# Linear attention with a gated feed-forward: reciprocal denominators replicated through DRAM, and half-chunk products of two pairs of tiles in one array mode

## The chip, the cores and the metric

The kernel runs on one core of a Trainium2 chip. The metric is device time in microseconds, the median of several executions. All executions quoted here are fast, at a mean granted TensorE clock of 0.99 to 1.00. A ratio is the mean time of one kernel's fast runs over the mean of the other kernel's fast runs of the same rounds, so it is not quite the ratio of the medians that stand beside it.

## The reference, cut to what matters

```python
xn = _layernorm(x)                                  # x: 1 x 2048 x 640, bf16
q, k, v = split_heads(xn @ wqkv)                    # 32 heads of 20
phi = lambda t: where(t > 0, t + 1, exp(t)) + 1e-6
kv  = einsum("bhsd,bhse->bhde", phi(k), v)
z   = einsum("bhsd->bhd", phi(k))
num = einsum("bhqd,bhde->bhqe", phi(q), kv)
den = einsum("bhqd,bhd->bhq", phi(q), z)[..., None] + 1e-6
s   = merge_heads(num / den) @ wo
g   = silu(relu(xn @ w1) @ w2)                      # w1: 640 x 1728, w2: 1728 x 640
return x + s * g
```

Two facts matter. The division by `den` is one number per head and token, and the kernel applies it to phi(q), whose 640 features lie on partitions: each of the 32 reciprocals has to be repeated over the 20 features of its head. And 1728 is 13 x 128 + 64, so the product with `w2` has a last chunk of 64 rows, half of the array.

## The kernel before

A small scheduler gives every operation a count on its engine and makes readers and overwriters wait for counts. If PE writes a bank that an earlier counted group of PE wrote, and nothing has told PE since that this group is done, PE waits for its own count.

In what follows PE is TensorE, DVE is VectorE, ACT is ScalarE, POOL is GpSimd, and SP is the engine that issues the DMAs. A bank is one of the eight 512-column pieces of PSUM, into which PE writes. A full matmul uses all 128 rows of the array. Blocks are named after their result: an H block is five matmuls of the product with `w1`, a G block is xn^T phi(k) for 128 features, a kv block multiplies that by the weights of v, and a W block multiplies kv by `wo`.

Features on partitions (`pqT`, phi(q) transposed, five chunks of 128), then the denominators. `den` leaves the reciprocals of 32 heads and 4 blocks of 512 tokens on 128 partitions (`rden`). They are spread to features by a matmul with a 0/1 matrix, one 32-row matmul per token block, and multiplied into `pqT` by DVE:

```python
def expand(m):
    fns = [(lambda eng, i=i: eng.matmul(ps[4 + i], lhsT=EmQ[H * i:H * (i + 1), m, :],
                                        rhs=rden[H * i:H * (i + 1), :], start=True, stop=True)) for i in range(J)]
    sc.group("PE", fns, ...)
    for i in range(J):
        sc.op("DVE", lambda eng, i=i: eng.tensor_tensor(out=pqT[:, m, schunk(i)], in0=pqT[:, m, schunk(i)],
                                                        in1=ps[4 + i], op=ALU.mult), ...)
...                                   # [cut]
for k in range(C):                    # C = 5
    lastG = G_block(k, gb[k % 2])     # 32 full matmuls: xn^T phi(k)
    expand(k)
```

The gate. `U(p)` computes the product with `w2` for a pair of token tiles, then four 64-row half products (two token tiles x two halves of the output), then two Silus. Output tiles (`s_tile`) of the previous pair run between its parts:

```python
def U(p, hook=None):
    ...                                                          # [cut: 26 full matmuls per output half n]
        if n == 0:
            sc.group("PE", fns, R=Rh, W=[("ps", bs[0]), ("ps", bs[0] + 1)])
            if hook is not None:
                hook()
    for n in range(2):
        for u in range(2):
            fns.append(lambda eng, u=u, n=n: eng.matmul(
                ps[bs[n] + u][:, 0:HN], lhsT=hTl[64 * u:64 * (u + 1), jp, P * q:P * (q + 1)],
                rhs=w2l[64 * u:64 * (u + 1), HN * n:HN * (n + 1)], start=False, stop=True))
    sc.group("PE", fns, R=..., W=[("ps", bs[n] + u) for n in range(2) for u in range(2)])
    for n in range(2):
        ...                                                      # [cut: Silu of output half n on ACT]
```

## Time and profile before

| | before |
|---|---|
| median time | 229.53 us |
| profiled span | 227.5 us |
| PE busy | 97% |
| share of PE in the chain that ended last | 93% |
| DVE, ACT, POOL busy | 47%, 39%, 20% |

Three lines of the page of the kernel before: span, busy time by engine (share of the span, number of instructions), and the chain that ended last by engine.

```profile
span 227.5 us, 3552 instructions
...
PE 221.0 (97%) x1474; PEld 134.8 (59%) x1484; DVE 108.1 (47%) x202; ACT 88.1 (39%) x145; POOL 46.1 (20%) x63
...
PE 93%; DVE 3%; DMA 2%; issue 1%; POOL 0%; SPq 0%; ACT 0%
```

PE is the limit. Only what shortens its stream of instructions, or the few microseconds after it, can shorten the run.

The chain in order of time (start, us, what) of the kernel before, at the expansions. L692 is a G block, L680 an expansion, L742 the first product with `w2`.

```profile
112.47 4.45 PE psT L692 x32
116.92 0.33 PE psT L680 x4
117.25 4.45 PE psT L692 x32
...
136.04 0.33 PE psT L680 x4
136.37 3.64 PE psT L742 x26
```

One G block and one expansion repeat every 4.78 us. At the steady pitch of full 320-column matmuls (26 in 3.53 us, 0.1358 us each) 32 of them take 4.345 us, so an expansion costs 0.435 us, not the 0.33 of its own line.

The timeline of the kernel before at one group of half products (L752); PEld is the weight load, in brackets the idle time before it and what ended it.

```profile
167.96 0.11 PEld L752 LDWEIGHTS psT<-reg,hTl 64*128 64x128 bf16 x4 [0.26 <-issue]
167.97 0.45 PE L752 MATMUL psT<-reg,hTl 64*128 64x320 bf16 x4
168.34 0.52 PEld L770 LDWEIGHTS psT<-reg,pqT 128*128 128x128 bf16 x5 [0.26 <-issue]
```

Weight loads otherwise follow each other closely (16.2 us of idle before the 416 loads of L742, 0.04 us each on the mean); going into the 64-row mode and coming out of it they stand idle for 0.26 us each time. The chain gives the price of the whole group. A pair of tiles repeats every 10.27 us, and its 72 full matmuls take 72 x 0.1358 = 9.78, so a group of four costs 0.48 us, or 0.96 us for two groups:

```profile
168.03 0.38 PE psT L752 x4
...
178.30 0.38 PE psT L752 x4
```

The timeline of the kernel before at its end: L770 are the last two output tiles, L759 the two Silus of the last pair, L784 the gate multiply, L787 the last add of the residual.

```profile
221.02 2.89 PE L770 MATMUL psT<-reg,pqT 128*128 128x320 bf16 x20
221.13 1.30 ACT L759 ACTIVATE reg<-psT 128x640 bf16<-128x640 f32 x2 [10.32 <-PE psT L752]
222.59 0.82 DVE L784 TENSOR_TENSOR reg<-psT,reg 128x640 bf16<-128x640 f32 x1 [4.02 <-PE psT L770]
...
225.14 0.32 DVE L787 TENSOR_TENSOR reg<-reg 128x320 bf16<-128x320 bf16 x1
```

From the start of the last products to the end of the last add: 225.14 + 0.32 - 221.02 = 4.44 us.

### The profile page before, as it was taken

Reading aid. Unit: us, or ns where it says so; the run is one execution under the profiler, and the core shown is the slowest. Engines: PE = TensorE matmul, PEld = TensorE weight load, DVE = VectorE, ACT = ScalarE, POOL = GpSimd, SP = SyncE. Lnnn points to the kernel's source line nnn. Section 1 sums busy time; section 2 is a strip of 40 time slices with the busy share of each in tenths; the row PEclk is TensorE's granted clock in tenths of the full one; section 3 lists DMA queues with packets and bytes.
Section 4 is the critical chain, followed back from the end, with each engine's and each line's share of the span. In section 5 each row is a group of like instructions: output and inputs, shape, how many; then the busy total and the mean of one; then the engine's idle time right before and its main releaser. Section 6 shows DMA issues by size and latency. Waiting matters only on the chain.

```text
span 227.5 us, 3552 instructions
## 1 busy us (share of the span) xinstructions
PE 221.0 (97%) x1474; PEld 134.8 (59%) x1484; DVE 108.1 (47%) x202; ACT 88.1 (39%) x145; POOL 46.1 (20%) x63
## 2 busy tenths in 40 slices
PE   7899999999999999999999999999999999999993
PEld 7664555455554555444466667666767676676762
DVE  3799911896549852945134446111323222222244
ACT  2898665567665667554511122322020202021011
POOL 2357642312632267700000004000000000000000
PEclk9999999999999999999999999999999999999999
DMA  6999900012401160000097009400100011000011
GB/s 206 325 397 232 242 4 0 0 30 58 32 1 29 29 61 22 0 0 3 5 331 214 0 0 297 168 0 3 58 32 29 29 55 35 29 29 32 29 58 58
DMA packets 20895, 17.95 MB, mean 79 GB/s; under 512 B 8880, under 2 KB 20880, under 8 KB 20880
## 3 DMA queue, kind: packets, MB, share of 16 engines
q1 hardware_dynamic: 20880, 17.74, 27.8%
q8 instruction: 11, 0.18, 0.4%
q14 instruction: 4, 0.03, 0.0%
HBM read 13.03 MB, written 2.62 MB: 69 GB/s over the span
## 4 chain that ended last, share of the span: by engine, by line
PE 93%; DVE 3%; DMA 2%; issue 1%; POOL 0%; SPq 0%; ACT 0%
PE psT L742 25%; PE psT L514 24%; PE psT L692 10%; PE psT L491 9%; PE psT L770 9%; PE psT L439 8%; DMA reg<-in_A_x_dram 2%; PE psT L719 2%; PE psT L752 1%; DVE stats L394 1%; PE psT L527 1%; DVE reg L784 1%; PE psT L680 1%; PE psT L704 1%; PE psT L602 1%
## 5 line engine op out<-in xcount | busy, mean ns | idle before, releaser
L742 PE MATMUL psT<-reg,hT 128*128 128x320 bf16 x416 | 59.1, 299 | 0.1
L514 PE MATMUL psT<-reg 128*128 128x512 bf16 x252 | 56.8, 379 | 0.5 <-issue 0.2
L742 PEld LDWEIGHTS psT<-reg,hT 128*128 128x128 bf16 x416 | 40.5, 98 | 16.2 <-PE psT L742 0.4
L514 PEld LDWEIGHTS psT<-reg 128*128 128x128 bf16 x260 | 25.3, 98 | 29.2 <-issue 0.4
L784 DVE TENSOR_TENSOR reg<-psT,reg 128x640 bf16<-128x640 f32 (+1 forms) x17 | 13.3, 784 | 54.2 <-PE psT L770 54.2
L518 ACT ACTIVATE hT<-psT 128x512 bf16<-128x512 f32 x52 | 31.0, 598 | 18.6 <-PE psT L514 18.3
L759 ACT ACTIVATE reg<-psT 128x640 bf16<-128x640 f32 x16 | 10.4, 700 | 70.9 <-PE psT L752 70.9
L451 POOL TENSOR_TENSOR zacc<-zacc,reg 128x640 f32<-128x640 f32 x16 | 22.6, 1411 | 19.9 <-DVE reg L470 19.5
L439 PE MATMUL psT<-reg 128*128 128x320 bf16 x160 | 24.4, 299 | 0.4 <-ACT reg L427 0.4
L770 PE MATMUL psT<-reg,pqT 128*128 128x320 bf16 x160 | 23.9, 299 | 0.0
L692 PE MATMUL psT<-reg 128*128 128x320 bf16 x160 | 22.6, 299 | 0.0
L491 PE MATMUL psT<-reg 128*128 128x512 bf16 x98 | 21.8, 379 | 0.1
L684 DVE TENSOR_TENSOR pqT<-pqT,psT 128x512 bf16<-128x512 bf16 x20 | 12.4, 682 | 17.7 <-PE psT L680 17.7
L439 PEld LDWEIGHTS psT<-reg 128*128 128x128 bf16 x160 | 15.4, 98 | 8.5 <-ACT reg L427 0.7
L770 PEld LDWEIGHTS psT<-reg,pqT 128*128 128x128 bf16 x160 | 15.1, 98 | 7.4 <-issue 1.8
L692 PEld LDWEIGHTS psT<-reg 128*128 128x128 bf16 x160 | 15.2, 98 | 7.0 <-issue 1.3
L491 PEld LDWEIGHTS psT<-reg 128*128 128x128 bf16 x100 | 9.8, 98 | 11.1
L394 DVE BATCH_NORM_STATS2 stats<-reg 128x6 f32<-128x320 bf16 x32 | 14.0, 479 | 3.4 <-DMA reg<-in_A_x_dram 3.4
L498 ACT ACTIVATE er<-psT 128x512 bf16<-128x512 f32 x20 | 12.2, 611 | 8.1 <-PE psT L491 3.5
L456 ACT ACTIVATE ek<-psT 128x640 bf16<-128x640 f32 x16 | 11.3, 707 | 9.1 <-PE psT L439 9.1
L468 DVE TENSOR_SCALAR ek<-ek 128x640 bf16<-128x640 bf16 x16 | 5.2, 328 | 19.3 <-ACT ek L456 19.3
L508 DVE SCALAR_TENSOR_TENSOR pqT<-er 128x512 bf16<-128x512 bf16 x15 | 12.9, 859 | 0.5
(63 smaller groups left out, 143.6 us busy)
## 6 DMA issues: line engine op xcount, KB each, us to landing
reg<-in_A_x_dram SPq DMA_DIRECT2D x16, 160.0 KB, 5.2
reg<-in_A_x_dram SPq DMA_DIRECT2D x4, 640.0 KB, 6.8
out_dram<-reg SPq DMA_DIRECT2D x15, 160.0 KB, 1.8
reg<-in_B_w_dram SPq DMA_DIRECT2D x2, 1120.0 KB, 7.4
reg<-in_B_w_dram SPq DMA_DIRECT2D x1, 1040.0 KB, 11.0
reg<-in_B_w_dram SPq DMA_DIRECT2D x1, 960.0 KB, 8.6
reg<-in_A_wqkv_dram SPq DMA_DIRECT2D x1, 800.0 KB, 5.3
wv_sb<-in_A_wqkv_dram SPq DMA_DIRECT2D x1, 800.0 KB, 5.2
```

The costliest lines, as they stand in the source:

```text
L394: sc.op("DVE", lambda eng, a=a: eng.bn_stats(stats[:, t, a, :], xv[:, HN * a:HN * (a + 1)]), R=[("xin", t % XR)], W=[("stats", t, a)])
L439: fns.append(lambda eng, a=a, k=k: eng.matmul(ps[b + a][:, 0:HN], lhsT=xnT[:, k, tok(t)], rhs=wqk[:, k, D + HN * a:D + HN * (a + 1)], star ...
L451: sc.op("POOL", lambda eng: eng.tensor_tensor(out=zacc[:, :], in0=zacc[:, :], in1=pk[:, t, :], op=ALU.add), R=[("zacc",), ("pk", t)], W=[( ...
L491: sc.group("PE", [(lambda eng, k=k: eng.matmul(ps[b], lhsT=wqk[:, k, P * f:P * (f + 1)], rhs=xnT[:, k, schunk(j)], start=(k == 0), stop=(k ...
L508: sc.op("DVE", lambda eng: eng.scalar_tensor_tensor(out=pqT[:, f, schunk(j)], in0=e_, scalar=1.0, in1=r_, op0=ALU.min, op1=ALU.add), R=[(" ...
L514: a = sc.group("PE", [(lambda eng, k=k: eng.matmul(ps[b], lhsT=w1_sb[:, k, P * f:P * (f + 1)], rhs=xnT[:, k, schunk(j)], start=(k == 0), s ...
L518: sc.op("ACT", lambda eng: eng.activation(out=hT[:, f, schunk(j)], in_=ps[b], func=ACTF.Relu), R=[("ps", b)], W=[("hT", j, f)])
L684: sc.op("DVE", lambda eng, i=i: eng.tensor_tensor(out=pqT[:, m, schunk(i)], in0=pqT[:, m, schunk(i)], in1=ps[4 + i], op=ALU.mult), R=[("ps ...
L692: fns.append(lambda eng, t=t, a=a: eng.matmul(ps[b + a][:, 0:HN], lhsT=xn[:, t, P * k:P * (k + 1)], rhs=pk[:, t, HN * a:HN * (a + 1)], sta ...
L742: fns.append(lambda eng, u=u, t=t, f=f, n=n: eng.matmul(ps[bs[n] + u][:, 0:HN], lhsT=hT[:, f, tok(t)], rhs=w2_sb[:, f, HN * n:HN * (n + 1) ...
L770: sc.group("PE", [(lambda eng, c=c, a=a: eng.matmul(ps[b + a][:, 0:HN], lhsT=pqT[:, c, tok(t)], rhs=wf[:, c, HN * a:HN * (a + 1)], start=( ...
L784: sc.op("DVE", lambda eng: eng.tensor_tensor(out=tmpo[:, os_, lo:hi].rearrange(shp, a=na), in0=src, in1=g_sb[:, t, lo:hi].rearrange(shp, a ...
```

## The change

It takes the replication of the reciprocals away from PE: four stores write each row of `rden` twenty times to a DRAM scratch of 640 x 2048, five loads bring it back with features on partitions (into the space of the transposed input, which is dead by then), and DVE multiplies 2048 columns at once. The denominators move three blocks earlier to give the transfers time. Half products of pair p and p + 1 are computed together, at the end of p, so the array changes its mode half as often. Both last output tiles, not only the last one, are evacuated in two halves.

```diff
-    EmQ = nc.alloc_sbuf_tensor("EmQ", [P, C, P], bf)
+    rx = xnT
+    rxd = nc.dram_tensor("rden_by_feature", [D, S], bf).ap()
@@ den
+        for i in range(J):
+            dma("SP", lambda eng, i=i: eng.dma_start(
+                rxd.rearrange("(h e) s -> h e s", e=DH)[:, :, schunk(i)],
+                rden[H * i:H * (i + 1), :].unsqueeze(1).to_broadcast([H, DH, 512])), R=[("rden",)], W=[("rxd", i)])
@@ order of the last H blocks
-                if n == 8:
+                if n == 7:
                     z_col()
-                if n == 12:
+                if n == 9:
                     den()
@@ after the loads of w2 and wo
+    for c in range(C):
+        dma("SP", lambda eng, c=c: eng.dma_start(rx[:, c, :], rxd[P * c:P * (c + 1), :]),
+            R=[("rxd", i) for i in range(J)], W=[("rx", c)], extra=[lastW1])
-    def expand(m):
-        ...
+    def divide(m):
+        return sc.op("DVE", lambda eng: eng.tensor_tensor(out=pqT[:, m, :], in0=pqT[:, m, :], in1=rx[:, m, :], op=ALU.mult), ...)
@@ U, for the even pair p, output half n = 1
+                sc.group("PE", fns + U_half(p, False), R=Rh + Rl, W=bk(0) + bk(1))
+                b2 = ubanks(p + 1)
+                W2 = [("ps", b2[i] + u) for i in range(2) for u in range(2)]
+                sc.group("PE", U_half(p + 1, True), R=Rl, W=W2)
@@ end
-        s_tile(t, last=(t == pairs[7][1]))
+        s_tile(t, last=True)
...                                   # [cut: banks, split evacuation of W, order of the output tiles]
```

`divide(0)` and `divide(1)` stand before the evacuations of the kv blocks on DVE, the other three behind them.

More of the change, by code (lines that the diff above doesn't have):

```diff
@@ L370, in build_consts @@
     def build_consts():
-        em = EmQ[0:H, :, :].rearrange("p c n -> p (c n)")
-        sc.op("POOL", lambda eng: eng.memset(em, 1.0), W=[("Em",)])
-        sc.op("POOL", lambda eng: eng.affine_select(out=em, in_=em, compare_op=ALU.is_ge, fill=0.0,
-                                                    base=0, pattern=[[1, D]], channel_multiplier=-DH),
-              R=[("Em",)], W=[("Em",)])
-        sc.op("POOL", lambda eng: eng.affine_select(out=em, in_=em, compare_op=ALU.is_ge, fill=0.0,
-                                                    base=DH - 1, pattern=[[-1, D]], channel_multiplier=DH),
-              R=[("Em",)], W=[("Em",)])
-        for qd in range(1, 4):
-            dma("SP", lambda eng, qd=qd: eng.dma_start(EmQ[H * qd:H * (qd + 1), :, :], EmQ[0:H, :, :]),
-                R=[("Em",)], W=[("Em4", qd)])
         sc.op("POOL", lambda eng: eng.memset(mh[:, :, :], 1.0), W=[("mh",)])
@@ L677, in nextp @@
         return b
-    def expand(m):
-        fns = [(lambda eng, i=i: eng.matmul(ps[4 + i], lhsT=EmQ[H * i:H * (i + 1), m, :], rhs=rden[H * i:H * (i + 1), :],
-                                            start=True, stop=True)) for i in range(J)]
-        sc.group("PE", fns, R=[("rden",), ("Em",)] + [("Em4", q) for q in range(1, 4)], W=[("ps", 4 + i) for i in range(J)])
-        for i in range(J):
-            sc.op("DVE", lambda eng, i=i: eng.tensor_tensor(out=pqT[:, m, schunk(i)], in0=pqT[:, m, schunk(i)],
-                                                            in1=ps[4 + i], op=ALU.mult),
-                  R=[("ps", 4 + i), ("pqT", i, m)], W=[("pqT", i, m)])
+    def divide(m):
+        return sc.op("DVE", lambda eng: eng.tensor_tensor(out=pqT[:, m, :], in0=pqT[:, m, :], in1=rx[:, m, :], op=ALU.mult),
+                     R=[("rx", m)] + [("pqT", i, m) for i in range(J)], W=[("pqT", i, m) for i in range(J)])
     def G_block(k, b):
@@ L722, in W_block @@
         sc.group("PE", fns, R=[("wo",), ("kvz",)] + [("kv", c) for c in cs], W=[("ps", b), ("ps", b + 1)])
-        if m % 2 == 0:
-            sc.op("ACT", lambda eng: eng.activation(out=wf[:, m, :].rearrange("p (a n) -> p a n", a=2), in_=ps2(b, HN),
-                                                    func=ACTF.Copy), R=[("ps", b), ("ps", b + 1)], W=[("wf", m)])
-        else:
-            sc.op("DVE", lambda eng: eng.tensor_copy(wf[:, m, :].rearrange("p (a n) -> p a n", a=2), ps2(b, HN)),
-                  R=[("ps", b), ("ps", b + 1)], W=[("wf", m)])
@@ L730, in bass_recurrent_scan__linear_attn_block__dense_activation_relu__prompt_kernel, with ubanks @@
-    pairs = [(4 * jj + q, 4 * jj + q + 4) for jj in (0, 2) for q in range(4)]
-    def U(p, hook=None):
+        sc.op("ACT", lambda eng: eng.activation(out=wf[:, m, 0:HN], in_=ps[b][:, 0:HN], func=ACTF.Copy),
+              R=[("ps", b)], W=[("wf", m, 0)])
+        sc.op("DVE", lambda eng: eng.tensor_copy(wf[:, m, HN:D], ps[b + 1][:, 0:HN]),
+              R=[("ps", b + 1)], W=[("wf", m, 1)])
+    pairs = [(4 * jj + q, 4 * jj + q + 4) for jj in (0, 2) for q in range(4)]
+    def ubanks(p):
+        return [4, 6] if p % 2 == 0 else [0, 2]
@@ L733, in U, with U_half @@
+    def U_half(p, start):
+        bs = ubanks(p)
+        jp, q = pairs[p][0] // 8, pairs[p][0] % 4
+        return [(lambda eng, u=u, n=n: eng.matmul(
+            ps[bs[n] + u][:, 0:HN], lhsT=hTl[64 * u:64 * (u + 1), jp, P * q:P * (q + 1)],
+            rhs=w2l[64 * u:64 * (u + 1), HN * n:HN * (n + 1)], start=start, stop=not start))
+            for n in range(2) for u in range(2)]
+    def U(p, hook):
         t0, t1 = pairs[p]
-        bs = [nextp(), nextp()]
+        bs = ubanks(p)
+        odd = p % 2 == 1
@@ L735, in U @@
         jp = t0 // 8
-        q = t0 % 4
         Rh = [("hT", t // 4, f) for t in (t0, t1) for f in range(NF)] + [("w2", 0), ("w2", 1)]
-        for n in range(2):
-            fns = []
-            for u, t in enumerate((t0, t1)):
-                for f in range(NF):
-                    fns.append(lambda eng, u=u, t=t, f=f, n=n: eng.matmul(
-                        ps[bs[n] + u][:, 0:HN], lhsT=hT[:, f, tok(t)], rhs=w2_sb[:, f, HN * n:HN * (n + 1)],
-                        start=(f == 0), stop=False))
-            if n == 0:
-                sc.group("PE", fns, R=Rh, W=[("ps", bs[0]), ("ps", bs[0] + 1)])
-                sc.allow_unread.update([("ps", bs[0]), ("ps", bs[0] + 1)])
-                if hook is not None:
-                    hook()
@@ L750, in U @@
-        for n in range(2):
-            for u in range(2):
-                fns.append(lambda eng, u=u, n=n: eng.matmul(
-                    ps[bs[n] + u][:, 0:HN], lhsT=hTl[64 * u:64 * (u + 1), jp, P * q:P * (q + 1)],
-                    rhs=w2l[64 * u:64 * (u + 1), HN * n:HN * (n + 1)], start=False, stop=True))
-        sc.group("PE", fns, R=Rh + [("hTl", jp), ("w2l", 0), ("w2l", 1)],
-                 W=[("ps", bs[n] + u) for n in range(2) for u in range(2)])
-        for n in range(2):
-            go = g_sb[:, t0:t0 + 5:4, HN * n:HN * (n + 1)]
-            sc.op("ACT", lambda eng, go=go, n=n: eng.activation(out=go, in_=ps2(bs[n], HN), func=ACTF.Silu),
-                  R=[("ps", bs[n]), ("ps", bs[n] + 1)], W=[("g", t0, n), ("g", t1, n)])
+        Rl = [("hTl", 0), ("hTl", 1), ("w2l", 0), ("w2l", 1)]
@@ new lines, in bk, with silu @@
+        def bk(n):
+            return [("ps", bs[n]), ("ps", bs[n] + 1)]
+        def silu(n):
+            go = g_sb[:, t0:t0 + 5:4, HN * n:HN * (n + 1)]
+            sc.op("ACT", lambda eng: eng.activation(out=go, in_=ps2(bs[n], HN), func=ACTF.Silu),
+                  R=bk(n), W=[("g", t0, n), ("g", t1, n)], extra=[divs[c] for c in sorted({v // S for t in (t0, t1) for v in (D * t, D * t + D - 1)})])
+        for n in range(2):
+            fns = [(lambda eng, u=u, t=t, f=f, n=n: eng.matmul(
+                ps[bs[n] + u][:, 0:HN], lhsT=hT[:, f, tok(t)], rhs=w2_sb[:, f, HN * n:HN * (n + 1)],
+                start=(f == 0 and not odd), stop=(f == NF - 1 and odd)))
+                for u, t in enumerate((t0, t1)) for f in range(NF)]
+            if n == 0 or odd:
+                sc.group("PE", fns, R=Rh, W=bk(n))
+                sc.allow_unread.update(bk(n))
+                if odd:
+                    silu(n)
+            else:
+                sc.group("PE", fns + U_half(p, False), R=Rh + Rl, W=bk(0) + bk(1))
+                b2 = ubanks(p + 1)
+                W2 = [("ps", b2[i] + u) for i in range(2) for u in range(2)]
+                sc.group("PE", U_half(p + 1, True), R=Rl, W=W2)
+                sc.allow_unread.update(W2)
+                silu(0)
+                silu(1)
+            if n == 0:
+                hook()
@@ L772, in s_tile @@
                 start=(c == 0), stop=(c == C - 1))) for c in range(C)],
-                R=[("pqT", i, c) for c in range(C)] + [("wf", c) for c in range(C)], W=[("ps", b + a)])
+                R=[("pqT", i, c) for c in range(C)] + [("wf", c, a) for c in range(C)], W=[("ps", b + a)])
         def piece(lo, hi, pin, addE="DVE"):
@@ L801, in bass_recurrent_scan__linear_attn_block__dense_activation_relu__prompt_kernel @@
         lastG = G_block(k, gb[k % 2])
-        expand(k)
+    divs = [divide(m) for m in range(2)]
     sc.op("POOL", lambda eng: eng.memset(kvp, 0.0), W=[("kvz",)], extra=[lastG])
@@ L808, in kv_all, with w_all, s_hook, f @@
     def kv_all():
-        b0, b1 = nextp(), nextp()
-        for c, b in enumerate((b0, b0 + 1, b1, b1 + 1, b0)):
+        for c, b in enumerate((0, 1, 2, 3, 0)):
             kv_block(c, b)
-    pr[0] = 1
-    U(0, kv_all)
-    pr[0] = 3
-    for m in range(C):
-        W_block(m)
-    for p in range(1, 8):
-        a, b = pairs[p - 1]
-        if p == 1:
-            U(p)
-            s_tile(a)
-            s_tile(b)
-        elif p < 7:
-            U(p, lambda: s_tile(a))
-            s_tile(b)
-        else:
-            U(p, lambda: (s_tile(a), s_tile(b)))
-    pr[0] += 2
+        for m in range(2, C):
+            divs.append(divide(m))
+    def w_all():
+        pr[0] = 2
+        for m in range(C):
+            pr[0] = 2 + m % 2
+            W_block(m)
+    def s_hook(ts, b0):
+        def f():
+            for i, t in enumerate(ts):
+                pr[0] = b0 // 2 + i % 2
+                s_tile(t)
+        return f
+    U(0, kv_all)
+    U(1, w_all)
+    for p in range(2, 8):
+        ts = pairs[p - 2] if p < 7 else pairs[5] + pairs[6]
+        U(p, s_hook(ts, 0 if p % 2 == 0 else 4))
+    pr[0] = 2
     for t in pairs[7]:
-        s_tile(t, last=(t == pairs[7][1]))
+        s_tile(t, last=True)
     sc.wait_all_dma("SP", list(range(nds[0])))
```

## The prediction

> **What bounds it now.** TensorE. The page gives PE 97% busy of a 227.5 us span, and the chain of waits is 93% PE, at a granted clock of 1.00. DVE (47%), ACT (39%) and the DMA engines (28%) have slack. So only what leaves PE's instruction stream, or the last few microseconds, can shorten the run; work taken from DVE or POOL is worth nothing by itself.
>
> **What is removed, from the timeline.**
> 1. Five groups of four 32-row matmuls (the expansion of the reciprocals). The stretches from one 32-matmul G group to the next repeat every 4.78 us; 32 such matmuls at their steady pitch (26 take 3.53 us, 0.1358 us each) need 4.345. Each expansion so costs 0.435 us: about 0.22 of streaming and as much again for two changes of the array's tile shape (the Trainium skill, "TensorEngine Tiling (Array Packing)", Key Properties: changing the mode drains TensorE; the 0.26 us holes before weight loads at each change agree). 5 x 0.435 = 2.2 us, all on the chain.
> 2. The 64-row half products. A pair of token tiles repeats every 10.26 us = 72 full matmuls (9.78) + 0.48; two concurrent rounds need 0.27, so 0.21 is the two mode changes. Eight entries become four: 4 x 0.21 = 0.8 us. The arithmetic stays.
> 3. The tail. Before, both Silus (1.3 us) come after the last half product, and the first of the two last tiles is a whole 640-wide piece: 4.44 us from the last products' start to the last DVE add. After, only one Silu (0.7 us) is left and all four pieces are halves: about 0.95 + 4 x 0.77 = 4.0. Worth 0.4 us.
>
> Sum 3.4 us. Also gone: 12.4 us of DVE multiplies and 2 us of POOL set-up, off the chain.
>
> **What is added.** Four broadcast stores (2.6 MB, 1 KB rows, from 32 partitions each), five loads (2.6 MB, 4 KB rows), five DVE multiplies of 2048 columns: the 320- and 640-wide bf16 adds take 325 and 492 ns, so an estimate of 1.23 us each (the skill's "VectorE: DVE Perf Modes", perf-mode tier table, has 1.224 us). The denominator product moves three H blocks earlier: rden should be ready at about 105.7 us instead of 108.8; POOL's z split ends at 95.8, before its product at 97.9, so no new wait.
>
> Are the loads in time? Estimates: stores 107.5 to 118-120; w2 and wo (3 MB at the 290 GB/s seen between 118 and 124 us) to about 129; rx0 and rx1 at about 132, the last at about 137. The first output group (now at about 134) needs w2; the kv evacuations (about 138) sit behind divisions 0 and 1 on DVE; the first s tile needs all of pqT only near 155. Everything fits, by 5 us for w2 and rx1.
>
> **Predicted: 226.1 us** (ratio 0.985), 225.3 to 228.5 in 8 of 10. Faster by over 2%: 0.10; within 2%: 0.83; slower: 0.07.
>
> **What would show it.** G groups back to back, 160 matmuls in about 21.8 us; four half groups of eight at about 0.75 us each with their changes; PE without a wait between 112 us and the last products; last DVE op about 4.0 us after the last products start; stores landed before 121, rx all before 138; divisions near 1.23 us.
>
> **What would make it wrong.** Stores at half the rate (32 partitions, DRAM as target): then w2, queued behind them, lands after 134 and PE stalls several microseconds; or rx1 lands late and DVE holds the kv evacuations. A wait of Silu on the divisions, or of the W products on only two pairs of banks, would cost tenths. If mode changes cost less when grouped differently, item 2 is off by tenths.

## The result

| | before | after |
|---|---|---|
| median of 5 runs | 229.53 us (229.41 to 230.09) | 226.54 us (226.36 to 227.22) |
| ratio | | 0.9873 (0.9854 to 0.9893) |
| profiled execution: time, span | 229.28, 227.5 us | 226.36, 224.9 us |

The prediction was 226.1 us in a range of 225.3 to 228.5. The same lines of the page, after:

```profile
span 224.9 us, 3511 instructions
...
PE 219.2 (97%) x1464; PEld 136.1 (61%) x1464; DVE 102.7 (46%) x192; ACT 88.5 (39%) x147; POOL 43.5 (19%) x60
...
PE 94%; DVE 3%; ACT 1%; POOL 1%; issue 1%; POOLq 0%; DVEq 0%
```

The chain of the changed kernel at the same place (L685 is now a G block, L751 a product with `w2`): 160 full matmuls without a break, and the next product at its steady 3.53 us.

```profile
112.56 21.84 PE psT L685 x160
134.40 3.53 PE psT L751 x26
```

Its timeline at one group of half products (L729):

```profile
164.24 0.39 PEld L729 LDWEIGHTS psT<-reg,hTl 64*128 64x128 bf16 x8 [0.26 <-issue]
164.24 0.72 PE L729 MATMUL psT<-reg,hTl 64*128 64x320 bf16 x8
...
165.02 0.52 PEld L751 LDWEIGHTS psT<-reg,hT 128*128 128x128 bf16 x5 [0.40 <-PE psT L729]
```

There are eight products for one entry, as intended. But the exit is not like before: the weight load behind them is idle for 0.40 us, not 0.26, and what ended it is PE itself. The whole stretch of idle, products and exit: groups of eight start every 20.45 us (164.31 to 184.76 in the chain), and the 144 full matmuls of that period take 144 x 0.1358 = 19.55, so a group costs 0.90 us where two groups of four cost 0.96. The prediction had 0.75.

```profile
164.31 0.67 PE psT L729 x8
...
184.76 0.67 PE psT L729 x8
```

Its timeline at the end (L779 the last tiles, L747 now one Silu, L793 multiply, L796 add):

```profile
218.43 2.88 PE L779 MATMUL psT<-reg,pqT 128*128 128x320 bf16 x20
218.63 0.70 ACT L747 ACTIVATE reg<-psT 128x640 bf16<-128x640 f32 x1 [8.26 <-PE psT L751]
219.44 0.49 DVE L793 TENSOR_TENSOR reg<-psT,reg 128x320 bf16<-128x320 f32 x1 [2.99 <-ACT reg L747]
...
222.25 0.33 DVE L796 TENSOR_TENSOR reg<-reg 128x320 bf16<-128x320 bf16 x1
```

4.15 us from the last products to the last add, and the first multiply now waits for ACT. What was added, on DVE (L678 the divisions, L700 the evacuations of kv):

```profile
132.46 2.51 DVE L678 TENSOR_TENSOR pqT<-pqT,reg 128x2048 bf16<-128x2048 bf16 x2 [26.79 <-DMA reg<-rden_by_feature]
...
138.28 1.56 DVE L700 TENSOR_TENSOR reg<-psT,mh 128x140 bf16<-128x140 f32 x5 [3.30 <-PE psT L697]
...
139.75 3.49 DVE L678 TENSOR_TENSOR pqT<-pqT,reg 128x2048 bf16<-128x2048 bf16 x3
```

The first two divisions end at 134.97 us and the evacuation behind them starts at 138.28, waiting for PE. So 3.3 us were to spare.

Where the 2.92 us of the two profiled executions lie (starts from the timelines, the last column the difference):

| stretch | before | after | saved |
|---|---|---|---|
| to the first G block | 112.40 | 112.50 | -0.10 |
| G blocks (and expansions) to the first kv block | 27.44 | 25.27 | 2.17 |
| kv blocks to the last output tiles | 81.18 | 80.66 | 0.52 |
| last output tiles to the last DVE add | 4.44 | 4.15 | 0.29 |
| last add to the end of the time | 3.82 | 3.78 | 0.04 |

The span alone would mislead in the last rows: with the trace's finer spans (227.54 and 224.91 us) time minus span is 1.74 us before and 1.45 after, while span end minus last add is 2.08 and 2.33. Only their sum is steady, so the last row is taken to the end of the time.

### The profile page after: what moved, and what is told of

The parts are those of the page before. It is cut to its first block, busy times and chain, and to the rows that moved or that the text cites. A ratio compares the mean times of both kernels' runs of the same rounds, so it can differ in the third digit from the quotient of the medians.

```text
span 224.9 us, 3511 instructions
## 1 busy us (share of the span) xinstructions
PE 219.2 (97%) x1464; PEld 136.1 (61%) x1464; DVE 102.7 (46%) x192; ACT 88.5 (39%) x147; POOL 43.5 (19%) x60
## 4 chain that ended last, share of the span: by engine, by line
PE 94%; DVE 3%; ACT 1%; POOL 1%; issue 1%; POOLq 0%; DVEq 0%
PE psT L751 25%; PE psT L505 25%; PE psT L685 10%; PE psT L482 10%; PE psT L430 8%; PE psT L779 8%; PE psT L367 2%; PE psT L712 2%; PE psT L729 1%; PE psT L518 1%; DVE reg L793 1%; DVE stats L385 1%; PE psT L697 1%; PE psT L593 1%; DVE reg L796 0%
## 5 line engine op out<-in xcount | busy, mean ns | idle before, releaser
L751 PE MATMUL psT<-reg,hT 128*128 128x320 bf16 x416 | 58.7, 299 | 0.3
L505 PE MATMUL psT<-reg 128*128 128x512 bf16 x260 | 58.6, 379 | 0.0
L751 PEld LDWEIGHTS psT<-reg,hT 128*128 128x128 bf16 x416 | 40.3, 98 | 17.0 <-PE psT L729 1.6
L747 ACT ACTIVATE reg<-psT 128x640 bf16<-128x640 f32 x16 | 10.8, 702 | 68.8 <-PE psT L729 35.4
L793 DVE TENSOR_TENSOR reg<-psT,reg 128x640 bf16<-128x640 f32 (+1 forms) x18 | 13.5, 749 | 49.0 <-PE psT L779 46.0
L430 PE MATMUL psT<-reg 128*128 128x320 bf16 x160 | 24.4, 300 | 0.0
L779 PE MATMUL psT<-reg,pqT 128*128 128x320 bf16 x160 | 22.9, 299 | 0.0
L482 PE MATMUL psT<-reg 128*128 128x512 bf16 x100 | 22.2, 379 | 0.0
L685 PE MATMUL psT<-reg 128*128 128x320 bf16 x160 | 21.9, 299 | 0.0
L685 PEld LDWEIGHTS psT<-reg 128*128 128x128 bf16 x160 | 15.6, 98 | 6.4 <-issue 0.4
L779 PEld LDWEIGHTS psT<-reg,pqT 128*128 128x128 bf16 x160 | 15.7, 98 | 6.1
L678 DVE TENSOR_TENSOR pqT<-pqT,reg 128x2048 bf16<-128x2048 bf16 x5 | 5.9, 1220 | 26.8 <-DMA reg<-rden_by_feature 26.8
```

What stands on the lines that cost most here:

```text
L430: fns.append(lambda eng, a=a, k=k: eng.matmul(ps[b + a][:, 0:HN], lhsT=xnT[:, k, tok(t)], rhs=wqk[:, k, D + HN * a:D + HN * (a + 1)], star ...
L482: sc.group("PE", [(lambda eng, k=k: eng.matmul(ps[b], lhsT=wqk[:, k, P * f:P * (f + 1)], rhs=xnT[:, k, schunk(j)], start=(k == 0), stop=(k ...
L505: a = sc.group("PE", [(lambda eng, k=k: eng.matmul(ps[b], lhsT=w1_sb[:, k, P * f:P * (f + 1)], rhs=xnT[:, k, schunk(j)], start=(k == 0), s ...
L685: fns.append(lambda eng, t=t, a=a: eng.matmul(ps[b + a][:, 0:HN], lhsT=xn[:, t, P * k:P * (k + 1)], rhs=pk[:, t, HN * a:HN * (a + 1)], sta ...
L751: fns = [(lambda eng, u=u, t=t, f=f, n=n: eng.matmul(ps[bs[n] + u][:, 0:HN], lhsT=hT[:, f, tok(t)], rhs=w2_sb[:, f, HN * n:HN * (n + 1)], ...
L779: sc.group("PE", [(lambda eng, c=c, a=a: eng.matmul(ps[b + a][:, 0:HN], lhsT=pqT[:, c, tok(t)], rhs=wf[:, c, HN * a:HN * (a + 1)], start=( ...
```

## The experiments

What the traces leave open is why a group of eight half products costs 0.90 us. Theory A: PE waits for its own count. The four products that open the next pair are a counted group, and the 26 full matmuls behind them add into the same banks, so the scheduler makes PE wait until that count is up, though the result is correct without this wait too (the second run below). Theory B: leaving the 64-row mode costs more by itself, because the next product adds into the banks just written, or after eight products instead of four. The other questions: are the parts of the change independent and as large as predicted, and how much slack had the data path that went off the chain?

### The changed kernel again

> The changed kernel once more, on the same chip as the next three, so that they can be set against it. Expected 226.5 us, 0.987 of before. In its profile the 20.45 us from one group of eight half products to the next (144 full matmuls at 0.1358 us are 19.55) should come again, so 0.9 us for one group with its changes of mode, where the prediction had 0.75.

226.32 us, ratio 0.9864 (0.9851 to 0.9876). Groups of eight start every 20.45 us again (164.55 to 185.00).

### Half products and the following matmuls in one counted group

```diff
+            if n == 0 and odd:
+                sc.group("PE", U_half(p, True) + fns, R=Rh + Rl, W=bk(0) + bk(1))
-                sc.group("PE", U_half(p + 1, True), R=Rl, W=W2)
```

> The four half products that open the next pair become part of the same counted group as the full matmuls behind them, so PE no longer waits for its own completion count between them. Theory A (the missing 0.15 us of each group of eight is that wait on PE's own count: the idle time of the weight load behind it is 0.40 us there and 0.26 us at the other mode changes): that idle time falls to 0.26, the period from group to group falls from 20.45 to about 20.3, the run is 0.5 us shorter than the changed kernel (226.0 us). Theory B (leaving the 64-row mode straight into a product that adds into the same banks, or after eight instead of four, costs more by itself): period and time stay, 226.5 us.

225.94 us, ratio 0.9843 (0.9831 to 0.9856), 0.4 us less than the changed kernel on the same chip. Its timeline at the same group:

```profile
164.20 0.72 PE L729 MATMUL psT<-reg,hTl 64*128 64x320 bf16 x8
...
164.85 0.52 PEld L751 LDWEIGHTS psT<-reg,hT 128*128 128x128 bf16 x5 [0.26 <-issue]
```

The idle time is 0.26 us and no longer ended by PE; the stretch from the half products to the next full matmul is 0.65 us instead of 0.78, and the period 20.32 us. A group now costs 20.32 - 19.55 = 0.77 us, the predicted 0.75 but for 0.02:

```profile
164.27 0.65 PE psT L729 x8
...
184.59 0.65 PE psT L729 x8
```

The matmuls, their order, their banks and the accumulation into them are the same, so theory B falls. What is left is the wait, or something else that came with one counted group fewer; two runs below are about that.

### The replication alone

The kernel before with the new replication, everything else as it was.

> The kernel before with the replication through DRAM alone (expansion, its constants and its multiplies gone; half products, W evacuation and tail as before). The prediction has 2.2 us for this part: 227.4 us, 0.9905 of before, G groups back to back in 21.8 us. If the rival is right that part of the gain is given back by DMA waits of the first output group or the kv evacuations, it is above 227.8 us with a PE wait between 134 and 145 us.

227.36 us, ratio 0.9911 (0.9897 to 0.9925); the 160 G matmuls take 21.84 us. The prediction's 2.2 us for this part is 2.1 us here, with no wait of PE on a transfer.

### The half products and the tail alone

The changed kernel with the expansions put back (the last one in banks 2, 3, 6 and 7 instead of 4 to 7).

> The changed kernel with the expansion by matmuls put back (the last expansion in other banks, so that the first output group need not wait for its evacuation): shared half products, split W evacuation and the tail remain. The prediction has 0.8 + 0.4 us for them: 228.3 us. Read from the traces (20.45 against 20.52 us for two pairs, last products to last DVE add 4.15 against 4.44): 0.3 + 0.3 us, so 228.9 us. Both parts together should give the whole change if they are independent.

228.69 us, ratio 0.9972 (0.9954 to 0.999). One execution, the profiled one, was slower at 229.98 us, for a reason ahead of anything that the change touches: the x for the first LayerNorm statistics landed at 6.95 us (5.50 in the kernel before), and the first G block began 1.45 us later. With it this part is worth 0.6 us on the mean, without it 0.85.

From the start of the first G block to the end of the last add the chain leaves out that start. It takes 112.99 us in the kernel before, 110.83 with the replication alone, 112.17 here and 110.02 in the changed kernel. So the two parts save 2.16 and 0.82 us, 2.98 together, against 2.97 for the whole change: they are independent. This part is worth 0.8 us, not 1.2.

### The old tail

```diff
-        s_tile(t, last=True)
+        s_tile(t, last=(t == pairs[7][1]))
```

> The changed kernel, but with only the last of the two last tiles evacuated in two halves, as before. The prediction's third item is 0.4 us for tail and Silu order together; the traces show 4.15 against 4.44 us from the last products to the last DVE add. If the halved pieces bring it, this run is 0.2 to 0.3 us slower than the changed kernel (226.6 us where that has 226.3 on the last chip) and its stretch is about 4.4 us; if the single Silu brings it, the stretch stays near 4.15 us and the time at 226.3.

226.73 us, ratio 0.9886 (0.9871 to 0.99). From the last products (219.14 us) to the last add (223.57) it takes 4.43 us: as before the change, though there is only one Silu. The first multiply waits for PE and not for the Silu, which ends 0.66 us earlier:

```profile
220.70 0.82 DVE L793 TENSOR_TENSOR reg<-psT,reg 128x640 bf16<-128x640 f32 x1 [3.54 <-PE psT L779]
...
223.24 0.33 DVE L796 TENSOR_TENSOR reg<-reg 128x320 bf16<-128x320 bf16 x1
```

So the smaller first piece brought the 0.29 us. The shorter Silu brought nothing by itself, since the 640-wide multiply has to wait for both product halves anyway. The changed kernel was not run on this chip, so this is read from the stretch; the whole-run times can't separate 0.3 us here.

### The two quartets swapped

```diff
-                sc.group("PE", fns + U_half(p, False), R=Rh + Rl, W=bk(0) + bk(1))
-                sc.group("PE", U_half(p + 1, True), R=Rl, W=W2)
+                sc.group("PE", fns + U_half(p + 1, True), R=Rh + Rl, W=bk(1) + W2)
+                sc.group("PE", U_half(p, False), R=Rl, W=bk(0) + bk(1))
```

> The changed kernel with the two quartets of each group of eight in the other order: first the four that open the next pair, then the four that close this one. The count that the next full matmuls wait for is then reached one quartet (0.27 us) earlier, while the number of mode changes and the eight matmuls are the same. Theory A (PE's wait on its own count): as with one counted group, idle time of the weight load behind it 0.26 instead of 0.40 us, period 20.32 instead of 20.45 us, run 0.4 to 0.5 us shorter than the changed kernel (about 225.9). Theory B' (one counted group was faster for having fewer counted groups or other code, not for the wait): 226.3 us, period 20.45.

231.11 us, ratio 1.0068 (1.0055 to 1.0081): 5 us slower than expected. The experiment was badly built, and its timeline shows how:

```profile
162.59 3.71 PE L751 MATMUL psT<-reg,hT 128*128 128x320 bf16 x26 [0.92 <-DVE reg L793]
...
166.74 0.11 PEld L729 LDWEIGHTS psT<-reg,hTl 64*128 64x128 bf16 x4 [0.40 <-PE psT L729]
167.12 3.37 PEld L751 LDWEIGHTS psT<-reg,hT 128*128 128x128 bf16 x26 [0.26 <-issue]
```

Waits stand in front of a whole counted group. By putting the quartet for the next pair into the group of the 26 full matmuls, I made those matmuls wait for the evacuation of banks that only the quartet needs (0.92 us here, 2.8 us in three such places). The chain from the first G block to the last add is 4.25 us longer than in the changed kernel: each of the three periods that contain such a wait is 1.2 us longer, the stretch before the first group of eight, where PE waits in the same way for the evacuations of kv, is 0.56 us longer, and the end 0.1. The second and third lines still speak for theory A: the exit is back at 0.26 us, and the 0.40 us on PE's own count has moved between the quartets, where this version asks for it. The time says nothing about A.

### Swapped, in three counted groups

The same order, with the 26 matmuls, the opening quartet and the closing quartet each counted by itself.

> The swapped order of the quartets again, but each counted by itself, so that the waits for the evacuations of the next pair's banks stand in front of the quartet that needs them and not in front of 26 full matmuls, as they did in the swapped version. There is one counted group more than in the changed kernel. Theory A (PE's wait on its own count, set just before): every count that is waited for was reached at least one quartet (0.27 us) earlier, so the idle time of the weight loads is 0.26 at entry and exit, the period is 20.32 us and the run about 225.9 us. Theory B' (fewer counted groups helped): 226.3 us or more, period 20.45.

226.17 us, ratio 0.9846 (0.9833 to 0.986), close to the one-group version's 0.9843 (another chip, each against the kernel before on its own). The line of the exit:

```profile
165.40 0.39 PEld L751 LDWEIGHTS psT<-reg,hT 128*128 128x128 bf16 x4 [0.26 <-PE psT L729]
```

The period is 20.31 us (164.83 to 185.14). There is one counted group more than in the changed kernel and the next full matmul still asks for a count of PE, but one that was reached a quartet earlier, and the extra 0.14 us of the period is gone. The number of groups is not the cause.

### The denominators where they were before

> The changed kernel with the denominator products where they stood before the change, three H blocks later: reciprocals, stores and loads come 3.2 us later. In the changed kernel the first two divisions ended at 135.0 us and the first kv evacuation behind them began at 138.3 us, so the slack is 3.3 us: if the data path really is off the chain by that much, the time is within 0.3 us of the changed kernel (226.3 to 226.6) and the divisions end at about 138.2 us.

226.86 us, ratio 0.9887 (0.9871 to 0.9903), and 226.35 us in the profiled run. The changed kernel was not run on this chip, and the ratios (0.9887 here, 0.9873 and 0.9864 there) leave up to about 0.5 us open. The chain closes that: from the first G block to the last add it takes 110.00 us here and 110.02 in the changed kernel. The divisions end 0.7 us before the evacuation that stands behind them:

```profile
135.07 2.50 DVE L678 TENSOR_TENSOR pqT<-pqT,reg 128x2048 bf16<-128x2048 bf16 x2 [26.16 <-DMA reg<-rden_by_feature]
...
138.27 1.56 DVE L700 TENSOR_TENSOR reg<-psT,mh 128x140 bf16<-128x140 f32 x5 [0.70 <-PE psT L697]
```

So the earlier denominators, a part of the change, bought slack and no time that these traces show.

### The denominators after the last H block

> The changed kernel with the denominator products after the last H block, 8.6 us later than in the changed kernel. If the slack is 3.3 us as read from the trace, the first two divisions end at about 143.6 us, the kv evacuations wait for them, PE waits some 4 to 5 us for the bank of the first kv block, and the run takes 230.5 to 231.5 us. If the time moves by less than 1 us, the divisions and loads have much more slack than read; if it moves by the whole 8.6 us they have none.

231.25 us, ratio 1.007 (1.0053 to 1.0086), 4.7 us slower than the changed kernel's 226.54.

```profile
137.39 5.04 PE L751 MATMUL psT<-reg,hT 128*128 128x320 bf16 x26 [2.83 <-DMA reg<-in_B_w_dram]
141.43 2.51 DVE L678 TENSOR_TENSOR pqT<-pqT,reg 128x2048 bf16<-128x2048 bf16 x2 [26.85 <-DMA reg<-rden_by_feature]
...
144.20 0.48 PE L697 MATMUL psT<-reg,wv_sb 128*128 128x140 bf16 x5 [0.51 <-DVE reg L700]
```

The size came as expected, the place only in part. From the first G block to the last add the profiled run takes 115.02 us, 5.0 more than the changed kernel. Most of it, 2.83 us, is PE waiting for the load of `w2`, which is issued behind the stores on the same queue. Another 1.35 us is clock: about 2.2 us into this wait the granted clock fell to 0.50 and stayed there for 3.4 us (136.7 to 140.2), so the 26 matmuls behind it took 4.88 us to the next product instead of 3.53. Only then does the path through the divisions show, with 0.85 us: the last kv block waits for the evacuation of its bank, which stands behind the two divisions. This is the way in which the prediction said that it might fail. Somewhere between 3.2 and 8.6 us of delay the gain is lost.

### Finer waits in the tail

On top of the one-group version: each half piece waits for its half of the gate only.

```diff
-                op=ALU.mult), R=keys + [("g", t, 0), ("g", t, 1)], W=kk("tmpo"))
+                op=ALU.mult), R=keys + [("g", t, h) for h in (0, 1) if lo <= HN * h < hi], W=kk("tmpo"))
```

> The one-group version, and each half piece of the tail waits only for the half of the gate that it multiplies: the first half's Silu is done long before. First multiply 0.8 us after the last products start (1.01 in the changed kernel), last DVE add 3.95 us after it (4.15). Expected 0.2 us below the one-group version: about 225.7 us.

225.73 us, ratio 0.9832 (0.9819 to 0.9846), the lowest ratio of all kernels here, though its interval overlaps that of the one-group version. The first multiply no longer waits for ACT, starts 0.88 us after the last products (217.81), and the last add ends 4.02 us after them, where the one-group version has 4.15.

```profile
218.69 0.49 DVE L793 TENSOR_TENSOR reg<-psT,reg 128x320 bf16<-128x320 f32 x1 [2.86 <-PE psT L779]
...
221.50 0.33 DVE L796 TENSOR_TENSOR reg<-reg 128x320 bf16<-128x320 bf16 x1
```

### Two adds of the tail on POOL

```diff
-            piece(0, HN, b)
+            piece(0, HN, b, "POOL")
```

> As the run with the finer gate waits, and the adds of the first half of both last tiles go to POOL, so that DVE has four multiplies and two adds in the tail. Last DVE add about 3.65 us after the last products start, POOL's adds (estimate 0.7 us, half of the 1.41 us of its 640-wide fp32 adds) end before it. Expected 0.5 us below the one-group version: about 225.4 us, 0.982 of before. If POOL's add takes over 1.2 us it ends last and nothing is gained over the finer waits.

226.09 us, ratio 0.9848 (0.9835 to 0.9862): no gain. The tail on the engines did get shorter, 3.86 us, and POOL's add took 0.79 us, but the time from the last add to the end grew from 3.77 to 4.07 us.

```profile
220.19 2.25 SPq L799 DMA_DIRECT2D out_dram<-reg  x4
...
220.83 0.79 POOL L796 TENSOR_TENSOR reg<-reg 128x320 bf16<-128x320 bf16 x1 [0.66 <-DVE reg L793]
221.37 0.42 DVE L796 TENSOR_TENSOR reg<-reg 128x320 bf16<-128x320 bf16 x1
```

POOL's second add ends at 221.62 us and DVE's last at 221.79, so two stores become ready 0.17 us apart, and SP needs 0.33 to 0.43 us to issue each: its last issue ends at 220.19 + 2.25 = 222.44 us. In the run with the finer waits it ended at 222.19.

### Seven more stores

The kernel before with seven middle output stores split in two, for the 0.3 us between span and time.

> The kernel before, with seven of its middle output stores split in two: seven DMA instructions more and nothing else. In all runs so far time minus profiled span is either 1.75 us (before, each half of the change, the old tail) or 1.45 us (the changed kernel and its variants); the SP queue holds 65, 66, 71 and 71 instructions in the former and 72 in the latter. If that length decides it, this kernel shows 1.45 us, with 229.1 us in place of 229.4; if it is something else in the change, 1.75 us and 229.4.

229.71 us, ratio 1.0008 (0.9996 to 1.0021), and 1.75 to 1.88 us between span and time. The length of the queue is not it. Why the recorded span ends later relative to the last add in some kernels was not found. It costs no time, since the sum of the two gaps stays at 3.8 us.

## Why the prediction was right or wrong

1. *"Five groups of four 32-row matmuls ... 2.2 us, all on the chain."* Right. The stretch became 2.17 us shorter, and the replication alone was worth 2.1 us. Counting an expansion from G block to G block, with its two changes of mode, was what made it right; its own lines (0.33 us each) would have given 1.65. The division of the 0.435 us between streaming and mode changes was not tested.
2. *"Eight entries become four: 4 x 0.21 = 0.8 us."* The size was wrong. This was the step that failed: the saving in the changed kernel is 4 x (0.96 - 0.90), about 0.25 us. The stretch from the kv blocks to the last output tiles did save 0.52 us, but about 0.2 of that is something else: before, the second pair waited once for PE's own count between its two output halves (a line of the kernel before, below), and the new order puts the W blocks there. The estimate of the mode changes themselves was good, as the one-group version shows with 0.77 us per group; what was missing was a wait that the new grouping brought in. It could have been read from the scheduler's rules: a group that writes a bank which PE itself wrote last asks for that count.

```profile
152.70 3.37 PEld L742 LDWEIGHTS psT<-reg,hT 128*128 128x128 bf16 x26 [0.39 <-PE psT L742]
```

3. *"The tail ... Worth 0.4 us."* 0.29 us, and for one of the two reasons given. The first piece is half as wide; that one Silu fewer had to run did not help alone.
4. *Loads in time "by 5 us for w2 and rx1".* Right in effect. For w2 the size was right too: issued 7.9 us later (120.47 instead of 112.60 us, with the denominators after the last H block) it made PE wait 2.83 us, so about 5 were to spare. For rx1 it was too wide: the divisions had 3.3 us, and three blocks of delay (3.2 us) cost nothing that could be measured, while five more made PE wait. Stores at 108 to 120 us and divisions of 1.22 us came as estimated. For the divisions the Trainium skill ("VectorE: DVE Perf Modes", perf-mode tier table) has 1.224 us at this width, and the trace agrees.

The prediction said 3.4 us; 2.9 us came. The first item, two thirds of the sum, was right; the other two were too large, and the range allowed for that.

## What to carry to other kernels

Price an operation that changes the array's mode from the full matmul before it to the full matmul after it: a quarter of the 0.435 us of each expansion here was not in its own line. When work is regrouped, go through the waits that the new grouping creates, also those of an engine on itself; with one such wait (0.13 us, four times) the halved mode changes gained about 0.25 us, without it about 0.8. A stall can cost more than its own length: after the 2.83 us wait of the late denominators the granted clock was still 0.50, which cost another 1.35 us. Data that can be prepared elsewhere is free only while its whole queue is on time: here a transfer for one purpose delayed the load of the next weights before it delayed its own reader.

## What the Trainium skill lacked or had wrong

- "TensorEngine Tiling (Array Packing)", Key Properties: it says that changing the tiling mode drains TensorE, which the traces agree with, but gives no price. Here weight loads are idle 0.26 us at every entry into the 64-row mode and at every exit without a further wait (0.26 and 0.23 us around the 32-row groups). One entry and exit together cost about 0.23 us of PE time beyond the streaming, as an estimate: 0.77 us for eight half products, of which 0.54 us, four rounds of 0.1358, is taken as streaming.
- The same page, same place: its advice would gain from a warning that a wait on PE's own count at the exit adds to that. The idle time was 0.40 us instead of 0.26, and 0.13 us of PE time was lost at each of four places.
- "SBUF — State Buffer", Door 1: it says that partitions 0 to 31 reach only 8 of 16 ports, with about 218 GB/s as the limit. The stores, from 32 partitions each, are consistent with it: 212 and 215 GB/s between 108 and 112 us, when nothing else was in flight, then 350 GB/s for the loads that follow. No run separates this from the other traits of the stores (rows of 1 KB, DRAM as target). What that section lacks is how such a limit looks in a profile: the DMA share is 0.95 at the lower rate and so doesn't show it (windows of the changed kernel below: PE, PEld, DVE, ACT and POOL busy, clock, DMA share, GB/s).

```profile
108.00:110.00 2.00, 2.00 (x11) 0.85 (x9) 0.00 (x0) 1.19 (x2) 0.00 (x0) 1.00 0.95 212
110.00:112.00 2.00, 2.00 (x20) 0.97 (x20) 0.00 (x0) 1.07 (x2) 0.00 (x0) 1.00 0.95 215
...
122.00:126.00 4.00, 4.00 (x32) 2.88 (x30) 0.00 (x0) 0.36 (x2) 0.00 (x0) 1.00 1.04 350
```

- "DMA: Bandwidth & Descriptors", Anatomy of one DMA: it gives about 50 ns for the sequencer's dispatch, for DMAs of GpSimd. The section lists no issue time for a store from SP. The runs show 0.33 us for each, over the whole issue and so not the same span as those 50 ns; it is what put off the last store in the run with adds on POOL.
